# Packed attention with a top-1 mixture of experts: whole-row w1 loads, a new step order and a root on another engine in the first batch

## The chip, the cores and the metric

One core of a Trainium2 chip runs the kernel. The metric is device time in microseconds (us), from the first to the last instruction with what lies around them; the median of the runs counts.

## The reference

```python
def sm_attn(qq, kk, vv):                      # per batch and head
    s = scale * np.matmul(qq, kk.transpose(0, 1, 3, 2))
    s = s - np.max(s, axis=-1, keepdims=True)
    a = np.exp(s)
    a = a / (np.sum(a, axis=-1, keepdims=True) + 1e-09)
    return np.matmul(a, vv)
p_packed = sm_attn(p, k, v)                   # 32 packed rows
out = sm_attn(q, p_packed, p_packed)
# q, k, v: 8 batches x 8 heads x 576 x 64; p: 8 x 8 x 32 x 64
x = out as rows [4608, 512]
xn = x / (norm(x) + 1e-06);  en = emb / (norm(emb) + 1e-06)
logits = xn @ en.T / tau                      # 8 experts
expert = argmax(logits);  gate = softmax(logits)[expert]
out[row] = gate * (relu(x @ w1[expert]) @ w2[expert])
# w1: 8 x 512 x 1024, w2: 8 x 1024 x 512
```

## The kernel before

The kernel goes through eight batches of 576 rows. For each batch it computes the packed attention in two steps (att1: 32 packed rows per head against all keys, packed into the small matrices T, ppx and p1T; att2: the 576 queries against the 32 packed rows), and then one FFN with the one expert that `guess` finds for the whole batch. The expert's index is read into a register, and the loads of that expert's w1 (`load_w1`) and w2 (`load_w2`) are issued with it, by SyncE (SP) in batch 0 and by GpSimd (POOL) later on. Rows that chose another expert are counted (`gates_main`), and are computed again at the end only if there are any. Attention and FFN are folded together: since att2's result is a product of a softmax and packed rows, w1 is first multiplied with the packed rows (G, of heads in two groups of four), and the hidden layer is then a product of G with the softmax AT (`hidden`, items f0 to f7 for each half of the rows, first half hf=0). Matrices are kept in two parts, high and low (the low one is what rounding leaves), so that a product takes three passes at full speed; in batch 0's first half, `hidden` takes fp32 operands (g32, ats) directly.

The order of instructions on every engine is the order in which the program writes them (a manual schedule); generators are stepped by the FFN's loop. From batch 1 on, the FFN of batch b steps the attention of batch b+1 by a rule. In batch 0 a table of strings sets it: after item n of the FFN the letters of PLAN[n+1] are run, where q is a step of the start (`begin`), s a step of batch 0's own softmax, a a step of batch 1's attention, G a split of G into its parts on GpSimd, w a split of w2, r a step of batch 0's routing and g a step of its gates. `begin` loads the first batch, computes the guess early from a total, issues w1 and prefetches the following inputs on SP's queue. In it, the steps of batch 0's softmax follow two strings: ORDS, an order of steps (U unpack, B maximum, S shift, X exponential, T total, N normalise, R turn, H high half, L low half; 0 and 1 are the two halves of rows), and ENG, an engine for each of the steps S0, S1, N0, N1 and so on (v VectorE, p GpSimd).

Names and lines that matter below (numbers of the kernel before, and behind a stroke those of the changed one):

- L174/L175: inputs q, k, v on SP; L527/L530: the index into a register; L737/L743, L746: w1's DMAs; L745/L754: w2's DMAs.
- L815/L833: the products of w1 with the packed rows (`rows_w1`); L847/L852, L873: the items of `hidden`; L851, L852: their evacuation into hT by ScalarE and VectorE.
- L891/L920: the FFN's last product, 96 of it to the end of a batch, and L875/L904 its remainder of 64 rows.
- L410/L419 and L424/L433: turn and logits of the packed rows of batch 1, through T (L481/L484, VectorE); L514/L517: its guess on TensorE; L251/L260: scores; L780/L789: rows of w1 of the next batch.
- L554, L559, L565, L574 to L576, L580, L589, L599 (L557, L562, L568, L577 to L579, L583, L592, L602): the steps of att2's softmax on VectorE: unpack, maximum, shift, total, normalise, turn, low half. ScalarE takes the exponential (L568/L571) and the high half (L595).
- L651/L659: routing products, of the high and low halves with ppx; ScalarE (L667) and VectorE (L660) evacuate.
- L98 to L113: one Newton step of a reciprocal root, called `rsqrt`; L710, L711 (L718, L719) end it for the gates, L713 (L721) is the reciprocal that follows, on VectorE.

The guess of batch 1 (letter a) sets when GpSimd may issue its w1, and w2 follows three steps of att2 later:

```python
yield from guess(x, 2 if b > 1 else 0)
load_w1(x, x.e, queue=nc.gpsimd)
second = att2(x, keys_main(b + 1) if b else None, b == 0, b < 1)
if b:
    for _ in range(3):
        yield next(second)
    load_w2(x, x.e, nc.gpsimd)
yield from second
```

## Time and profile before

| | |
|---|---|
| median of 3 runs | 448.43 us (448.02 to 448.60) |
| profiled execution | 448.61 us |
| its span, first to last instruction | 447.0 us |
| mean clock granted to TensorE | 0.993 |
| busy: TensorE, VectorE, ScalarE, GpSimd | 431.6, 306.7, 203.3, 145.4 us |
| HBM read and written | 78.00 MB, 9.44 MB |

The span is that of one profiled execution, and all positions are microseconds from its first instruction. Busy time says how much an engine did; where the kernel can become shorter is told by the chain that ended last (which follows, from the last instruction backward, what released each step) and by the timelines of single engines, which give idle time and what ended it.

### The profile page before, as it was taken

Reading aid. Unit: us, or ns where it says so; the run is one execution under the profiler, and the core shown is the slowest. Engines: PE = TensorE matmul, PEld = TensorE weight load, DVE = VectorE, ACT = ScalarE, POOL = GpSimd, SP = SyncE. Lnnn points to the kernel's source line nnn. Section 1 sums busy time; section 2 is a strip of 40 time slices with the busy share of each in tenths; the row PEclk is TensorE's granted clock in tenths of the full one; section 3 lists DMA queues with packets and bytes.
Section 4 is the critical chain, followed back from the end, with each engine's and each line's share of the span. In section 5 each row is a group of like instructions: output and inputs, shape, how many; then the busy total and the mean of one; then the engine's idle time right before and its main releaser. Section 6 shows DMA issues by size and latency. Waiting matters only on the chain.

```text
span 447.0 us, 10448 instructions
## 1 busy us (share of the span) xinstructions
PE 431.6 (97%) x3762; PEld 340.7 (76%) x3763; DVE 306.7 (69%) x1020; ACT 203.3 (45%) x477; POOL 145.4 (33%) x184
## 2 busy tenths in 40 slices
PE   7789989999999999999999999999999999999994
PEld 5537768789687968879687887879787886879784
DVE  4478778569883799459894699658994598535400
ACT  2456723475137722476226742377234751466110
POOL 2446733153404422043503423044401534035000
PEclk9999999999999999999999999999999999999998
DMA  7999979856994379933996279934799306500011
GB/s 213 277 278 279 241 208 339 260 126 166 297 352 137 107 217 363 293 105 91 289 374 183 78 207 332 316 102 111 229 366 271 87 1 210 226 26 23 15 48 54
DMA packets 40843, 88.22 MB, mean 197 GB/s; under 512 B 10376, under 2 KB 19912, under 8 KB 40784
## 3 DMA queue, kind: packets, MB, share of 16 engines
q1 hardware_dynamic: 32496, 57.96, 45.4%
q0 software_dynamic: 8000, 29.43, 18.0%
q8 instruction: 32, 0.52, 0.5%
q14 instruction: 27, 0.22, 0.2%
q10 hardware_dynamic: 288, 0.08, 0.1%
HBM read 78.00 MB, written 9.44 MB: 196 GB/s over the span
## 4 chain that ended last, share of the span: by engine, by line
PE 90%; DMA 5%; SPq 1%; DVE 1%; ACT 1%; issue 0%; ACTq 0%
PE pf L891 41%; PE pf L847 23%; PE pf L875 7%; PE pt L651 7%; PE pt L251 4%; PE pt L780 3%; PE pt L381 3%; DMA nat<-in_q 2%; PE pt L361 2%; DMA w1t<-in_moe_w 2%; DMA nat<-in_v 2%; SPq L737 1%; PE pu L424 0%; ACT p L346 0%; PE pu L410 0%
## 5 line engine op out<-in xcount | busy, mean ns | idle before, releaser
L891 PE MATMUL pf<-w2s,hT 128*128 128x512 f32 (+1 forms) x792 | 190.0, 392 | 0.0
L891 PEld LDWEIGHTS pf<-w2s,hT 128*128 128x128 f32 x792 | 143.7, 190 | 38.1 <-issue 6.7
L756 POOL TENSOR_TENSOR w2s<-w2r,w2s 128x512 fp32r<-128x512 f32 x64 | 82.7, 1294 | 185.9 <-ACT w2s L755 185.3
L847 PE MATMUL pf<-AT,G 128*128 128x288 f32 x720 | 104.8, 299 | 0.0
L847 PEld LDWEIGHTS pf<-AT,G 128*128 128x128 f32 x720 | 97.6, 188 | 4.5 <-issue 2.8
L851 ACT ACTIVATE hT<-pf 128x224 fp32r<-128x224 f32 (+1 forms) x128 | 48.0, 388 | 46.0 <-PE pf L847 45.4
L852 DVE SCALAR_TENSOR_TENSOR hT<-pf,hT 128x224 fp32r<-128x224 f32 (+1 forms) x128 | 52.2, 411 | 15.2 <-ACT hT L851 14.8
L667 ACT ACTIVATE at<-pt 128x512 f32<-128x512 f32 (+1 forms) x40 | 23.9, 598 | 44.4 <-DVE lg L660 44.1
L755 ACT CAST w2s<-w2r 128x512 fp32r<-128x512 f32 x64 | 39.8, 624 | 1.2 <-issue 1.2
L1146 ACT ACTIVATE o<-pf,gate 128x512 f32<-128x512 f32 (+1 forms) x41 | 25.9, 635 | 30.1 <-PE pf L891 18.6
L651 PEld LDWEIGHTS pt<-ppx,AT 128*128 128x128 f32 (+1 forms) x240 | 33.0, 177 | 4.3 <-DVE p1T L375 0.4
L651 PE MATMUL pt<-ppx,AT 128*128 128x264 f32 (+1 forms) x240 | 35.5, 286 | 0.0
L660 DVE TENSOR_REDUCE lg<-pt 128x8 f32<-128x16 f32 (+1 forms) x40 | 6.8, 171 | 39.7 <-PE pt L651 39.7
L875 PE MATMUL pf<-w2r,h 128*64 128x256 f32 x256 | 33.9, 390 | 0.0
L281 DVE STREAM_TRANSPOSE kt<-nat 128x512 f32<-128x512 f32 x28 | 31.1, 1109 | 0.0
L794 DVE TENSOR_TENSOR G<-pt,G 128x512 fp32r<-128x512 f32 x28 | 18.8, 689 | 14.2 <-ACT G L793 14.2
L266 POOL TENSOR_TENSOR ppx<-pp,ppx 128x256 fp32r<-128x256 f32 x16 | 12.0, 773 | 40.5 <-ACT ppx L265 40.5
L568 ACT ACTIVATE st<-st 128x576 f32<-128x576 f32 (+1 forms) x17 | 11.2, 657 | 29.3 <-DVE st L565 28.6
L875 PEld LDWEIGHTS pf<-w2r,h 128*64 128x64 f32 x256 | 15.8, 136 | 9.9 <-issue 4.3
L745 POOL DMA_DIRECT2D w2r<-in_moe_w x28 | 19.8, 713 | 0.0
L595 ACT CAST AT<-at 128x576 fp32r<-128x576 f32 x16 | 10.7, 673 | 19.6 <-DVE at L589 19.6
L793 ACT CAST G<-pt 128x512 fp32r<-128x512 f32 x28 | 15.8, 588 | 7.1 <-DVE G L794 4.8
(172 smaller groups left out, 477.2 us busy)
## 6 DMA issues: line engine op xcount, KB each, us to landing
nat<-in_k SPq DMA_DIRECT2D x112, 140.0 KB, 3.3
nat<-in_q SPq DMA_DIRECT2D x112, 140.0 KB, 4.0
w1t<-in_moe_w POOLq DMA_DIRECT2D x14, 1024.0 KB, 7.3
w2r<-in_moe_w POOLq DMA_DIRECT2D x28, 512.0 KB, 10.6
out<-o SPq DMA_DIRECT2D x27, 256.0 KB, 2.8
nat<-in_v SPq DMA_DIRECT2D x32, 160.0 KB, 4.2
nat<-in_v SPq DMA_DIRECT2D x32, 128.0 KB, 4.1
w1t<-in_moe_w SPq DMA_DIRECT2D x8, 256.0 KB, 5.3
```

The costliest lines, as they stand in the source:

```text
L281: nc.vector.transpose(kt[:, :512].rearrange("p (c i a) -> p c a i", a=4, i=32), t[:, :16].rearrange("p (c a) d -> p c a d", a=4),)
L651: nc.tensor.matmul(pt[:r, 512 * g : 512 * g + XW], AT[:, a, g, c * P : c * P + r], x.ppx[:, m, g], start=(i == 0), stop=(i == 2),)
L667: nc.scalar.activation(scr[:r, :, : HB * D], ptv[:r, :, 0 : HB * D], AF.Square, accum_out=ss[:r, c : c + 1])
L745: queue.dma_start(t, w2e[:, 2 * i : 2 * i + 2, :])
L755: nc.scalar.copy(t[:, 0], raw)
L756: nc.gpsimd.tensor_tensor(out=t[:, 1], in0=raw, in1=t[:, 0].bitcast(F32), op=ALU.subtract)
L847: nc.tensor.matmul(pf[:, :HS], w, r, start=(n == 0), stop=(n == len(ops) - 1))
L851: nc.scalar.activation(hT[:, 0, f, cs], pf[:, :n], AF.Relu)
L852: nc.vector.scalar_tensor_tensor(out=hT[:, 1, f, cs], in0=pf[:, :n], scalar=0.0, in1=hT[:, 0, f, cs].bitcast(F32), op0=ALU.max, op1=ALU.su ...
L875: nc.tensor.matmul(pf[64 * hf : 64 * hf + 64, :256], h4[:, f], x.w2r[f // 2][:, f % 2, hf * 256 : hf * 256 + 256], start=(f == 0), stop=(f ...
L891: nc.tensor.matmul(pf[:, :w], hT[:, a, f, c * P : (c + 1) * P], x.w2s[f][:, m, at : at + w], start=(f == 0 and i == 0), stop=(f == NF - 1 ...
L1146: nc.scalar.activation(o[:, :w], pf[:, :w], AF.Copy, scale=x.gate[:, c : c + 1])
```

## The change

1. `load_w1` of batch 0 takes w1 as four DMAs of whole rows (128 x 1024, 512 KB each) instead of eight of half rows (256 KB each). One DMA of batch 1's keys (HELD) moves from ahead of the index load to behind w1's.
2. `rows_w1` goes by head group instead of by half of the columns. After group 0, four items of `hidden` (f0 to f3) are opened: their products with group 0 alone run first, in four banks of PSUM; then group 1 follows in a bank of another pool, and `hidden` adds the second products.
3. Batch 0's softmax: ORDS ends with H1 L1 H0 L0, and N1 moves from VectorE to GpSimd.
4. A new PLAN. Batch 0's row logits stand between L904's; T of batch 1 is copied ahead of its gates; more of L920 stands around the logits of batch 1 and ahead of its scores.
5. `att1` turns batch 1's second group one step later. `att2` of batch 1 runs its routing from inside (`early`), step by step in turn with the keys of batch 2, where before routing followed the keys.
6. `gates` takes an engine; for batch 0 its root (`rsqrt`, and the two operations behind it) goes to GpSimd.

```diff
+                if isinstance(b, int) and (b, n, e, h) == HELD:
+                    hold.append(move)
+                else:
+                    move()
...
+    HELD = (1, 1, 1, 1)
...
-    def att2(x, after=None, first=False, b1=False):
+    def att2(x, after=None, first=False, early=False):
...
+            if early:
+                steps = route(x)
+                yield next(steps)
+                low(1)
+                yield
+                yield from alternate(steps, after)
+                return
             yield
             low(1)
             yield from idle(2)
-
-        if b1:
-            yield from alternate(softmax(), after)
-        else:
-            yield from softmax()
             if after:
                 yield from after
...
-    def gates(x):
+    def gates(x, eng=nc.vector):
...
-        for n, _ in enumerate(rsqrt(ss, y, "g")):
+        for n, _ in enumerate(rsqrt(ss, y, "g", eng)):
             if n % 3 == 2:
                 yield
-        nc.vector.tensor_tensor(out=y, in0=y, in1=ss, op=ALU.mult)
-        nc.vector.tensor_scalar(out=y, in0=y, scalar1=1e-6, scalar2=None, op0=ALU.add)
+        eng.tensor_tensor(out=y, in0=y, in1=ss, op=ALU.mult)
+        eng.tensor_scalar(out=y, in0=y, scalar1=1e-6, scalar2=None, op0=ALU.add)
         yield
         nc.vector.reciprocal(y, y)
...
-        for hf in range(2):
-            for i in range(parts):
...
+        for i in range(NPR if whole else 2):
+            if whole:
+                queue.dma_start(w1t[:, i], w[:, i])
...
+        def rows_w1(g):
+            if g == 0:
+                for _ in range(2):
+                    x.g32.append(sb.tile([P, NG, 512], F32, name="g32", tag="w2s", bufs=NF))
+                pfs = [ps.tile([P, 512], F32, name="pf", tag="pf") for _ in range(2)]
+                order = [(fc, (2 * a, 2 * a + 1)) for a in range(2) for fc in range(2)]
+            else:
+                pt = pb.tile([P, 1024], F32, name="pt", tag="pb")
+                pfs = [pt[:, fc * 512 : fc * 512 + 512] for fc in range(2)]
+                order = [(fc, range(HB)) for fc in range(2)]
...
+        def first_half(f, g):
+            if g == 0:
+                opened[f] = ps.tile([P, 512], F32, name="pf", tag="pf")
+            nc.tensor.matmul(
+                opened[f][:, :HS], x.g32[f // 4][:, g, f % 4 * P : f % 4 * P + P],
+                x.ats[0][:, g], start=(g == 0), stop=(g == NG - 1),
+            )
...
-            for fc in range(2):
-                yield from rows_w1(fc)
+            yield from rows_w1(0)
+            for f in range(HB):
+                first_half(f, 0)
+            yield
+            yield from rows_w1(1)
...
-        second = att2(x, keys_main(b + 1) if b else None, b == 0, b < 1)
+        second = att2(x, keys_main(b + 1) if b else None, b == 0, b == 1)
...
-        if b:
+        if b > 1:
             yield from route(x)
...
-        load_w1(x, x.e, NPR)
+        load_w1(x, x.e, True)
+        hold.pop()()
...
-        yield from gates(x)
+        yield from gates(x, nc.vector if b else nc.gpsimd)
...
-    ORDS = "U0a B0a S0a X0a U0b B0b T0a S0b X0b T0b N0a N0b U1 R0a B1 S1 X1 R0b T1 N1 R1 H0 H1 L1 L0"
-    ENG = "pvpvppppvp"
+    ORDS = "U0a B0a S0a X0a U0b B0b T0a S0b X0b T0b N0a N0b U1 R0a B1 S1 X1 R0b T1 N1 R1 H1 L1 H0 L0"
+    ENG = "pvppppppvp"
...
-        "qssq", "sssssssssq", "ssqsssG", "ss", "", "ss", "sa", "asss", "a", "Gsq",
+        "qssq", "sssssssss", "sss", "ss", "sGs", "ss", "Gs", "ssa", "ssa", "qa",
...
```

Where instructions go is seen from each engine's own order. First TensorE at the start of batch 0's FFN (pf and pt are PSUM banks, at and g the fp32 softmax and G). Before:

```order
L815 MATMUL pf<-w1t,tw 32x512 x16
L847 MATMUL pf<-at,g_502 128x288 x8
L847 MATMUL pf<-at,g_530 128x288 x2
L424 MATMUL pu<-enT,T 64x8 x4
L847 MATMUL pf<-at,g_530 128x288 x6
L847 MATMUL pf<-AT,G 128x288 x12
```

And in the changed kernel:

```order
L833 MATMUL pf<-w1t,tw 32x512 x8
L852 MATMUL pf<-at,g_472 128x288 x4
L833 MATMUL pt<-w1t,tw 32x512 x8
L852 MATMUL pf<-at,g_472 128x288 x4
L852 MATMUL pf<-at,g_473 128x288 x8
L873 MATMUL pf<-AT,G 128x288 x12
```

Four products of the items, with group 0, now stand between the two halves of the w1 rows, and the logits (L424) have left this place.

Second, TensorE around the scores and the routing of batch 1, in the middle of the last product of batch 0's FFN. Before:

```order
L891 MATMUL pf<-w2s,hT 128x512 x6
L410 MATMUL pu<-ident,pp_966 128x128
L410 MATMUL pu<-ident,pp_968 128x128
L891 MATMUL pf<-w2s,hT 128x512 x3
L424 MATMUL pu<-enT,T 64x8 x4
L514 MATMUL pu<-m_1015,itau 1x8 x2
L251 MATMUL pt<-kt,T 32x288 x16
L891 MATMUL pf<-w2s,hT 128x512 x69
L651 MATMUL pt<-ppx,AT 128x264 x12
```

And in the changed kernel:

```order
L920 MATMUL pf<-w2s,hT 128x512 x6
L419 MATMUL pu<-ident,pp_961 128x128
L419 MATMUL pu<-ident,pp_963 128x128
L920 MATMUL pf<-w2s,hT 128x512 x6
L433 MATMUL pu<-enT,T 64x8 x4
L920 MATMUL pf<-w2s,hT 128x512 x3
L517 MATMUL pu<-m_1009,itau 1x8 x2
L260 MATMUL pt<-kt,T 32x288 x16
L920 MATMUL pf<-w2s,hT 128x512 x48
L659 MATMUL pt<-ppx,AT 128x264 x6
L920 MATMUL pf<-w2s,hT 128x512 x6
L659 MATMUL pt<-ppx,AT 128x264 x6
```

Six more products (12 and 3 instead of 9 in all ahead of the scores) stand around the logits L433, and the first routing product stands behind 48 of the last product instead of 69.

Third, GpSimd, from the last w1 DMA of batch 1 on. Before, where the root of batch 0's gates is on VectorE:

```order
L737 DMA w1t<-in_moe_w 128x4x512
L745 ISA
L745 DMA w2r<-in_moe_w 128x2x512
L745 ISA
L745 DMA w2r<-in_moe_w 128x2x512
L745 ISA
L745 DMA w2r<-in_moe_w 128x2x512
L745 ISA
L745 DMA w2r<-in_moe_w 128x2x512
L644 MEMSET lg 64x8
L645 MEMSET ss 64x1
```

And in the changed kernel, from the root's third operation of the last Newton step on (the two w1 DMAs and the two operations ahead of it are not shown):

```order
L112 TENSOR_SCALAR rq_t<-rq_t 128x5
L113 TENSOR_TENSOR gy<-rq_t,gy 128x5
L754 ISA
L754 DMA w2r<-in_moe_w 128x2x512
L754 ISA
L754 DMA w2r<-in_moe_w 128x2x512
L754 ISA
L754 DMA w2r<-in_moe_w 128x2x512
L754 ISA
L754 DMA w2r<-in_moe_w 128x2x512
L718 TENSOR_TENSOR gy<-gy,ss 128x5
L719 TENSOR_SCALAR gy<-gy 128x5
```

The root's last two operations (L718, L719) stand behind all DMA issues of batch 1's weights; nine operations of the root stand ahead of the index load.

Fourth, VectorE at the start of batch 1's softmax. Before:

```order
L554 STREAM_TRANSPOSE st<-pt 128x288 x2
L710 TENSOR_TENSOR gy<-gy,ss 128x5
L711 TENSOR_SCALAR gy<-gy 128x5
L559 TENSOR_REDUCE mx_1087<-st 128x18
L565 TENSOR_TENSOR st<-st,mx_1087 128x576
L554 STREAM_TRANSPOSE st<-pt 128x288 x2
L559 TENSOR_REDUCE mx_1094<-st 128x18
L713 RECIPROCAL gy<-gy 128x5
L714 TENSOR_TENSOR lg<-lg,gy 128x40
L574 TENSOR_REDUCE s_1099<-st 128x18
```

And in the changed kernel:

```order
L557 STREAM_TRANSPOSE st<-pt 128x288 x2
L562 TENSOR_REDUCE mx_1091<-st 128x18
L721 RECIPROCAL gy<-gy 128x5
L722 TENSOR_TENSOR lg<-lg,gy 128x40
L568 TENSOR_TENSOR st<-st,mx_1091 128x576
L557 STREAM_TRANSPOSE st<-pt 128x288 x2
L729 TENSOR_REDUCE gate<-lg 128x5
L730 TENSOR_SCALAR gate<-gate 128x5
L562 TENSOR_REDUCE mx_1114<-st 128x18
L732 RECIPROCAL gate<-gate 128x5
```

The reciprocal that takes the root's result (L713, now L721) came behind both maxima and now comes behind the first; shift and unpack of the second half stand behind it.

## Rows read from the trace of the kernel before

**Rows 1.** The page of the profile, its parts on the engines (busy time, share of the span, instructions) and the chain that ended last (shares of the span by engine):

```profile
PE 431.6 (97%) x3762; PEld 340.7 (76%) x3763; DVE 306.7 (69%) x1020; ACT 203.3 (45%) x477; POOL 145.4 (33%) x184
...
PE 90%; DMA 5%; SPq 1%; DVE 1%; ACT 1%; issue 0%; ACTq 0%
```

**Rows 2.** The chain that ended last, from 8 to 32 us: start in us, length in us, what ran (SPq is SyncE's queue):

```profile
9.22 8.44 DMA nat<-in_q
17.68 0.31 SPq L174
...
18.04 0.47 SPq L527
...
19.01 0.38 SPq L737
...
22.76 7.06 DMA w1t<-in_moe_w
```

**Rows 3.** The timeline of TensorE from 22 to 40 us: start, length (of all that are counted in xN), line, operation, shapes, and in brackets the idle time before it and what ended it:

```profile
23.29 1.06 PE L815 MATMUL pf<-w1t,tw 64*32 64x512 f32 x8
...
30.85 5.12 PE L847 MATMUL pf<-at,g 128*128 128x288 f32 x20
...
36.57 3.18 PE L847 MATMUL pf<-at,g 128*128 128x288 f32 x12 [0.27 <-ACT m L434]
```

**Rows 4.** The timeline of VectorE from 24 to 40 us, same columns:

```profile
26.85 0.44 DVE L589 STREAM_TRANSPOSE at<-st 128x288 f32<-128x288 f32 x1
...
30.90 0.76 DVE L580 TENSOR_TENSOR st<-st,s 128x576 f32<-128x576 f32 x1
```

**Rows 5.** The timeline of GpSimd from 8 to 40 us, same columns (the first two rows are the first and the last of 14 operations of the embeddings' root, one behind the other):

```profile
9.83 0.18 POOL L103 TENSOR_TENSOR rq_t<-rq_h,rq_i 8x1 f32<-8x1 f32 x1 [3.76 <-DVE rq_i L93]
...
13.32 0.20 POOL L139 TENSOR_SCALAR enrm<-enrm 8x1 f32<-8x1 f32 x1
...
25.23 0.67 POOL L580 TENSOR_TENSOR st<-st,s 128x288 f32<-128x288 f32 x1 [0.42 <-DVE s L576]
...
29.27 1.26 POOL L266 TENSOR_TENSOR G<-g,G 128x512 fp32r<-128x512 f32 x1
```

**Rows 6.** The timeline of TensorE from 57 to 66.5 us, same columns:

```profile
61.25 0.95 PE L891 MATMUL pf<-w2s,hT 128*128 128x512 f32 x3
63.29 0.41 PE L424 MATMUL pu<-enT,T 128*64 128x8 f32 x8 [1.10 <-DVE T L481]
63.98 0.24 PE L514 MATMUL pu<-m,itau 128*1 128x8 f32 x4 [0.28 <-DVE m L434]
...
65.28 1.84 PE L891 MATMUL pf<-w2s,hT 128*128 128x512 f32 x4
```

**Rows 7.** Windows of 1 us: busy time in all and of PE, PEld, DVE, ACT and POOL (instructions), the clock granted to TensorE (1.00 is 2.4 GHz), the DMA engines' share and GB/s:

```profile
65.00:66.00 1.00, 1.00 (x18) 0.63 (x3) 0.93 (x6) 0.00 (x0) 0.00 (x0) 0.79 0.73 200
66.00:67.00 1.00, 1.00 (x4) 0.74 (x3) 0.96 (x5) 0.00 (x0) 0.57 (x1) 0.50 0.01 4
...
68.00:69.00 1.00, 1.00 (x3) 0.78 (x3) 0.97 (x4) 0.68 (x1) 1.00 (x3) 0.50 0.77 143
69.00:70.00 1.00, 1.00 (x6) 0.78 (x5) 0.96 (x4) 0.00 (x0) 1.00 (x2) 1.00 1.03 418
```

**Rows 8.** The chain that ended last, over the whole span, its longer pieces: start, length, what ran:

```profile
65.35 17.79 PE pf L891 x69
83.14 1.48 PE pt L651 x12
...
90.48 2.99 PE pf L891 x12
...
116.47 16.24 PE pf L891 x69
```

**Rows 9.** The timeline of TensorE from 82 to 94 us, columns as in rows 3:

```profile
88.53 1.95 PE L780 MATMUL pt<-w1t,T 64*32 64x512 f32 x32 [0.33 <-ACT at L667]
```

**Rows 10.** The timeline of GpSimd from 60 to 75 us, columns as in rows 3:

```profile
66.43 1.58 POOL L737 DMA_DIRECT2D w1t<-in_moe_w  x2 [1.95 <-DVE gy L710]
68.00 2.83 POOL L745 DMA_DIRECT2D w2r<-in_moe_w  x4
70.88 0.10 POOL L644 MEMSET lg<- 64x8 f32 x1
```

**Rows 11.** The timeline of VectorE from 63 to 82 us, same columns:

```profile
64.76 0.14 DVE L521 CAST gi<-idx 1x1 f32<-1x1 uint32 x1
...
67.32 0.76 DVE L565 TENSOR_TENSOR st<-st,mx 128x576 f32<-128x576 f32 x1
...
69.54 0.18 DVE L713 RECIPROCAL gy<-gy 128x5 f32<-128x5 f32 x1
...
75.11 0.69 DVE L599 TENSOR_TENSOR AT<-at,AT 128x576 fp32r<-128x576 f32 x1
...
78.02 0.76 DVE L599 TENSOR_TENSOR AT<-at,AT 128x576 fp32r<-128x576 f32 x1 [0.74 <-ACT AT L595]
...
79.19 0.40 DVE L276 STREAM_TRANSPOSE kt<-nat 128x256 f32<-128x256 f32 x1
```

**Rows 12.** The view of the cores: span and mean clock granted to TensorE:

```profile
core 0: 447.0 us, clock 0.993
```

More of the change, by code (lines that the diff above doesn't have):

```diff
@@ L451, in pack @@
             turned = []
-            def turn(g):
+            for g in range(NG):
                 turned.append(pb.tile([P, 1024], F32, name="pt", tag="pb"))
                 p1_turn(x, g, turned[g], turned[g][:, 512:])
-            turn(0)
-            if tight:
-                turn(1)
-            yield from idle(gap)
-            if not tight:
-                turn(1)
+                if g == 0:
+                    yield
             for g in range(NG):
@@ L630, in softmax @@
             yield from idle(2)
-        if b1:
-            yield from alternate(softmax(), after)
-        else:
-            yield from softmax()
             if after:
                 yield from after
+        yield from softmax()
     def route(x):
@@ L806, in ffn @@
         h4 = sb.tile([P, NF, 64], F32, name="h4", tag="h4")
-        def rows_w1(fc):
-            fs = slice(fc * 512, fc * 512 + 512)
-            pfs = [ps.tile([P, 512], F32, name="pf", tag="pf") for _ in range(NG)]
-            for g in range(NG):
-                for c in range(HB):
-                    h = head(g, c)
+        def rows_w1(g):
[4 more added lines that the diff above has]
+                order = [(fc, (2 * a, 2 * a + 1)) for a in range(2) for fc in range(2)]
+            else:
+                pt = pb.tile([P, 1024], F32, name="pt", tag="pb")
+                pfs = [pt[:, fc * 512 : fc * 512 + 512] for fc in range(2)]
+                order = [(fc, range(HB)) for fc in range(2)]
+            for fc, hs in order:
+                for h in hs:
+                    c = head(g, h)
                     nc.tensor.matmul(
-                        pfs[g][32 * c : 32 * c + 32],
+                        pfs[fc][32 * c : 32 * c + 32],
                         half_rows(x.Tw, h)[:, g * P + 32 * c : g * P + 32 * c + 32],
-                        half_rows(x.w1t[:, 2 * g + h // 2], h)[:, fs],
+                        half_rows(x.w1t[:, 2 * g + h // 2], h)[:, fc * 512 : fc * 512 + 512],
                         start=True,
@@ L845, in hidden @@
                 ]
-            for n, (w, r) in enumerate(ops):
-                nc.tensor.matmul(pf[:, :HS], w, r, start=(n == 0), stop=(n == len(ops) - 1))
+                for n, (w, r) in enumerate(ops):
+                    nc.tensor.matmul(pf[:, :HS], w, r, start=(n == 0), stop=(n == len(ops) - 1))
             yield
@@ L863, in ffn @@
         if late:
-            for fc in range(2):
-                yield from rows_w1(fc)
+            yield from rows_w1(0)
+            for f in range(HB):
+                first_half(f, 0)
+            yield
+            yield from rows_w1(1)
         elif not hasattr(x, "w1g"):
```

36 lines of the change are left out of this document (16 added, 20 removed), and 3 rows, old and new, of the table PLAN.

## The prediction

> **What bounds the kernel now.** I read the page's shares first: TensorE is busy for 97% of the span and carries 90% of the chain that ended last [rows 1]. So what counts is time in which TensorE idles, or runs at the lower clock. The long pieces of that chain then show where: from batch 1 on, a batch repeats every 51.2 us with hardly a gap, and the change touches nothing there. What is left is batch 0 and the attention of batch 1 that runs beside its FFN, from 9 to 93.5 us.
>
> Three stretches have slack. First, the load: the chain goes from in_q's landing (9.22 + 8.44 = 17.66) over SP's index load to the w1 issues and ends with the landing of the last w1 piece at 22.76 + 7.06 = 29.82 [rows 2]; TensorE waits for w1 piece by piece until then, and the FFN's first item starts at 30.85 [rows 3]. Second, around 63 us: 1.10 us of idle before the row logits (for the T copy) and 0.28 us before the guess [rows 6]. Third, behind that idle time the granted clock stands at 0.50 from 66 to 69 us, the lower of the two levels (1.2 of 2.4 GHz) [rows 7]: the x69 stretch of the last product takes 17.79 us, where the same x69 in batch 1 takes 16.24 [rows 8]. That fall cost 1.55 us. All times below are on the clock of the profiled execution before (448.61 us with what lies around its 447.0 us span, 0.18 above the median of the runs), unless "after the early gain" is said.
>
> **The change, part by part.**
>
> *w1 as four whole-row DMAs, index load moved past one key DMA.* SP now reaches the w1 issue with the key DMA held back. Before, the index load began at 18.04 and the w1 issues came from 19.01 on, 8 of them until 22.76 [rows 2]. Four issues of the same kind, two of which together replace four of the old ones, are out by about 20. SP still has to wait for the DMA slot that in_q frees at 17.66, so the start comes earlier by at most the 19.01 - 18.25 = 0.75 us that the held DMA and its queue slot took. The bytes are the same 2 MB. I expect the last w1 at 28.3, some 1.5 us earlier: 0.75 from the start and as much from fewer, longer rows. The bounds: 29.8 (nothing gained) and 27.3.
>
> *By head group, with four items opened.* Products of group 0 need two of the four DMAs; then TensorE waits for the first half of the attention, that DVE turns at 26.85 + 0.44 = 27.29 [rows 4]. Four half items of 0.512 us (5.12 / 10; the trace shows two records to a product) [rows 3] run until 29.3, the eight products of group 1 (1.06 for four, and denser behind each other) until 31.1, and the other four halves until 33.1. Then the second half's attention (R1) is due. Its N1 moves from DVE, 0.76 us, to GpSimd, where 288 columns take 0.67, so two of them 1.35, behind the split of G at 1.26 (which comes at about 30.0) [rows 4, 5]: R1 ends at 33.4, and with the evacuation f4 can start at 33.85. Eight products of 0.512 end at 38.0. Before, the sixteen ended at 36.57 + 3.18 - a rest = 39.4 [rows 3], of which 0.41 was the logits of batch 0, that now stand later; there they cover a stall of 0.27. So the early part gains 39.4 - 38.0 - 0.41 + 0.27 = **1.3 us**. Bounds: 0.5, if w1 lands no earlier than before (group 1 then ends at 31.9), and 2.2, if GpSimd's N1 comes before the split.
>
> *The row logits of batch 1.* The T copy comes ahead of the gates' root on DVE and six more products stand in the idle time (15 instead of 9 of the 96 before the key scores). I get the end of the scores at 64.95 instead of 65.28, with 6 products of 16.24 / 69 = 0.235 us [rows 8] more done: 0.33 + 1.41 = 1.74 us gained. The clock then has no idle time to fall after, 1.55 us; and the 0.33 us that TensorE waited for an evacuation ahead of the weight rows at 88.53 [rows 9] is covered by products that now lie between the routing steps. Together 3.6 us, if nothing else moves.
>
> *The gates' root on GpSimd.* This is the part that decides. On GpSimd nine of the root's operations come first, then the index, two w1 DMAs, four more root operations, four w2 DMAs, and only then the last two, for which DVE's reciprocal waits. The index is ready at 64.76 + 0.14 on DVE [rows 11]; GpSimd's first w1 issue followed at 66.43, two took 1.58 and the four of w2 2.83 [rows 10]. Its next instruction, a memset, begins at 70.88, right at the end of the fourth (68.00 + 2.83): so GpSimd works through the issues one after the other and nothing passes them. In the new order the index is as early as before within 0.15 us, so the first issue begins at 66.3 and ends the second at 67.9. Four root operations at 0.27 each (14 of them took from 9.83 to 13.52 [rows 5]) make 69.0, the four issues 71.8, the last two operations 72.4.
>
> On DVE the reciprocal stands behind the first three operations of the softmax of batch 1, at 66.6, so DVE stands idle for about 5.8 us. Behind it are the shift, the second half's turn and maximum, that had been done ahead of it before (67.32 to 69.54 = 2.2 us), and then the chain that took from 69.54 to the end of the first low half at 75.11 + 0.69 = 75.80 (6.26 us), and to 78.02 + 0.76 = 78.78 for the second [rows 11]. 72.4 + 2.2 + 6.3 = 80.9 for the first low half. TensorE has 48 products after the scores: 64.95 + 48 x 0.235 = 76.25. Then comes the first routing product, which needs that low half. **TensorE waits 4.7 us**, until 81.0. Nothing else is in its queue that could run.
>
> After such a wait I expect what the rows of before show after 1.10 + 0.28 us of idle time: the clock at the lower level for some 3 us, 1.55 us lost [rows 6, 7]. I take 1.7; bounds 0 (it doesn't fall) and 2.6 (longer at the lower level, since what follows, 6-product groups between routing steps, is less dense than the x69).
>
> What is left from there: 33 products (7.8), 30 records of routing at 1.48 / 12 = 0.123 (3.7), the weight rows at 1.9 [rows 8, 9]: 13.35. The end of batch 0's part is 81.0 + 13.35 + 1.7 = 96.1 instead of 90.48 + 2.99 = 93.47: **2.6 us lost**. From there the kernel goes as before.
>
> *Edits that I cost at nothing:* the T of the first attention steps and the turn of batch 1 one step later, since the next of TensorE's products are in its queue beside them; and the keys of batch 2, spread between routing steps instead of standing ahead of them: DVE turned them from 79.19 on [rows 11], while the scores of batch 2 come only after the last product at 93.47; they now come some 5 to 10 us later, still ahead of that. If that cover were gone, TensorE would wait for them once, up to 1 us.
>
> **Sum:** -1.3 + 2.6 = +1.3 us, from the profile's 448.61 to 449.9, and from the median of 448.43 to **449.7 us**.
>
> **Rivals.**
>
> A. *The DMA issues don't hold GpSimd up.* If GpSimd is through six issues at little cost, the root's end comes 66.3 + 4 x 0.27 + 0.5 = 67.9, DVE waits 1.3 us, the first low half is there at 67.9 + 8.5 = 76.4, and TensorE runs through: it gains the 1.3 + 1.74 + 1.55 + 0.33 = 4.9, which makes 443.5. The point from which this decides: the root's end before 67.8 costs nothing; each microsecond later is one lost; with the clock's fall the change breaks even where it comes at 71.0. The rows speak against it: 0.7 to 0.8 us per issue and the memset only behind the last [rows 10]. The Trainium skill, "DMA: Bandwidth & Descriptors", section "Anatomy of one DMA — SWDGE (gpsimd) path", would have it this way: dispatch of some 50 ns, and descriptor generation "small, variable"; by it, an estimate, six issues take well under 1 us and the sum would be about 443.5 as well. The trace does not agree, with 2.83 us for four. Chance 0.11.
>
> B. *TensorE waits, but the clock does not fall,* or only for the few tenths in which little runs. The price of 1.7 is gone: 448.0, no change that can be told. For it: the granted clock is 0.993 over the whole span [rows 12], so the many other waits of TensorE did not make it fall. Against it: [rows 6, 7] fell after a shorter one. Also in this case lies a mean of A and the forecast, by 1 us less waiting on DVE since part of the shift's chain can overlap with ScalarE. Chance 0.27, a third of it under 447.5.
>
> C. *Slower still:* the early part gains nothing, because the held key DMA and w1's long rows share the DMA engines until 29.8, or because TensorE's short wait for R0 (26.6 to 27.3) makes the clock fall too, on a stretch that is on the chain. 449.7 + 1.3 to 449.7 + 2.1: 451.0 to 451.8. Chance 0.14.
>
> D. *The change doesn't do what it says:* w1 comes earlier but its use is set by R0 and R1 on DVE and GpSimd, so that early w1 buys less than I wrote, 0.5 instead of 1.3: 450.5. It counts with the forecast.
>
> **How the numbers follow.** The forecast has 0.48 (D within it), A 0.11, B 0.27, C 0.14. What a measurement of this kernel can tell from no change is 0.2%, 0.9 us: faster is under 447.5, slower over 449.3. Faster: A and a third of B, 0.20. Same: the rest of B and 0.10 of the forecast (where the fall costs 1.2 or less), 0.28. Slower: 0.38 + 0.14 = 0.52. The range takes in B down to 446.8 and C up to 451.8 and leaves out A and some of B. The likeliest case's own range is 449.0 to 450.8.
>
> **What would show it.** In the changed kernel: last w1 by 28.5 and four half items before 29.5; f4's start bound by DVE's evacuation of R1; no idle time before L433 of batch 1; a gap of 5 us and more on DVE ended by GpSimd before L721; on GpSimd L719 behind four L754 issues; a gap of 4 to 5 us on TensorE before the first L659 of batch 1, and 0.50 in the clock's rows behind it. If the gap on DVE is under 2 us, the forecast is wrong, and the step that failed is the issues' cost on GpSimd; if it is there and TensorE's gap is not, I have the place of the low half's need wrong.

## The result, and the profile after

The changed kernel takes 450.98 us (median of 7 runs, 449.62 to 451.85), the kernel before 448.04 us beside it (445.08 to 448.60). The ratio is 1.0076, 95% interval 1.0052 to 1.0099: slower by 2.3 to 4.4 us. The forecast was 449.7, range 446.8 to 451.8.

The profiled execution is the shortest of the seven (449.62 us, span 447.9). A second one, taken later, has a span of 448.8. The last product's long stretch in batch 1, which began at 116.47 before [rows 8], begins 1.9 us later in the one and 2.5 us later in the other. (The spans are only 0.9 and 1.8 us longer than the 447.0 before, in part because the profiled execution before has one later batch of 51.65 us, where its other batches take 51.2 to 51.3.) The chain that ended last, the first and the second execution of the changed kernel:

```profile
118.36 16.22 PE pf L920 x69
```

```profile
118.98 16.22 PE pf L920 x69
```

GpSimd's timeline of the changed kernel, from w1's issues on, answers to [rows 10]:

```profile
65.44 1.61 POOL L746 DMA_DIRECT2D w1t<-in_moe_w  x2 [1.20 <-issue]
...
67.95 0.20 POOL L113 TENSOR_TENSOR gy<-rq_t,gy 128x5 f32<-128x5 f32 x1
68.53 2.93 POOL L754 DMA_DIRECT2D w2r<-in_moe_w  x4 [0.38 <-issue]
71.48 0.21 POOL L718 TENSOR_TENSOR gy<-gy,ss 128x5 f32<-128x5 f32 x1
71.78 0.23 POOL L719 TENSOR_SCALAR gy<-gy 128x5 f32<-128x5 f32 x1
```

Two w1 issues take 1.61 us, four w2 issues 2.93 (1.58 and 2.83 before), and the root's last two operations begin right where the fourth issue ends. L719 ends at 72.01.

VectorE's timeline answers to [rows 11]:

```profile
72.04 0.19 DVE L721 RECIPROCAL gy<-gy 128x5 f32<-128x5 f32 x1 [5.96 <-POOL gy L719]
...
79.79 0.69 DVE L602 TENSOR_TENSOR AT<-at,AT 128x576 fp32r<-128x576 f32 x1
...
82.70 0.76 DVE L602 TENSOR_TENSOR AT<-at,AT 128x576 fp32r<-128x576 f32 x1 [0.74 <-ACT AT L598]
```

From 66.08 on it waits for L719, 5.96 us. The low halves (L602) then end at 80.48 and 83.46; before they ended at 75.80 and 78.78.

TensorE's timeline answers to [rows 6]:

```profile
61.75 0.41 PE L433 MATMUL pu<-enT,T 128*64 128x8 f32 x8
...
64.28 11.42 PE L920 MATMUL pf<-w2s,hT 128*128 128x512 f32 x48
79.48 0.51 PE L659 MATMUL pt<-ppx,AT 128*128 128x264 f32 x2 [3.78 <-ACT AT L598]
80.54 1.25 PE L659 MATMUL pt<-ppx,AT 128*128 128x264 f32 x4 [0.54 <-DVE AT L602]
81.58 2.45 PE L920 MATMUL pf<-w2s,hT 128*128 128x512 f32 x6
...
86.03 1.56 PE L920 MATMUL pf<-w2s,hT 128*128 128x512 f32 x6
...
92.24 3.06 PE L920 MATMUL pf<-w2s,hT 128*128 128x512 f32 x12
95.13 0.95 PE L873 MATMUL pf<-AT,G 128*128 128x288 f32 x6
```

The 1.10 and 0.28 us of idle time around the row logits (L433) are gone, as is the 0.33 of [rows 9]. In their place TensorE waits 3.78 us for the first routing product, whose last step ahead of it is ScalarE's high half, and 0.54 us more for VectorE's low half. The six products at 81.58 take 2.45 us, those at 86.03 only 1.56. Why, the windows of 1 us show (columns as in [rows 7]; the clock is the third number from the right):

```profile
80.00:81.00 1.00, 0.46 (x2) 0.47 (x3) 1.00 (x2) 0.00 (x0) 0.00 (x0) 0.56 0.00 0
81.00:82.00 1.00, 1.00 (x5) 0.92 (x5) 0.92 (x2) 0.01 (x1) 0.00 (x0) 0.50 0.00 0
...
83.00:84.00 1.00, 1.00 (x6) 0.82 (x5) 0.97 (x4) 0.62 (x2) 0.00 (x0) 0.73 0.00 0
84.00:85.00 1.00, 1.00 (x9) 0.96 (x8) 0.20 (x3) 0.32 (x2) 0.00 (x0) 1.00 0.57 131
```

The clock falls to 0.50 behind the wait, as it fell before behind the shorter one.

The start of batch 0's FFN on TensorE answers to [rows 3]:

```profile
22.12 3.09 PE L833 MATMUL pf<-w1t,tw 64*32 64x512 f32 x16 [0.27 <-DMA w1t<-in_moe_w]
25.93 2.18 PE L852 MATMUL pf<-at,g 128*128 128x288 f32 x8 [0.72 <-ACT g L843]
...
31.04 6.66 PE L852 MATMUL pf<-at,g 128*128 128x288 f32 x24 [0.68 <-ACT g L843]
...
45.49 0.71 PE L370 MATMUL pt<-ident,p 128*128 128x128 f32 x5
...
50.22 1.71 PE L659 MATMUL pt<-ppx,AT 128*128 128x264 f32 x12 [1.06 <-DVE p1T L384]
```

The first turn of batch 1 stands at 45.49 instead of 47.71, 2.2 us earlier. Then a wait that before did not have: 1.06 us for VectorE's copy of p1T. The first routing product of batch 0, at 51.27 before, starts at 50.22, in the second execution at 50.71. VectorE's timeline ahead of this copy (L384):

```profile
48.35 1.15 DVE L290 STREAM_TRANSPOSE kt<-nat 128x512 f32<-128x512 f32 x1
...
49.81 0.46 DVE L384 COPY p1T<-pt 64x128 f32<-64x128 f32 x2
```

### The profile page after: what moved, and what is told of

Read it like the earlier page. It is cut to its first block, busy times and chain, and to the rows that moved or that the text cites. A ratio compares the mean times of both kernels' runs of the same rounds, so it can differ in the third digit from the quotient of the medians.

```text
span 447.9 us, 10440 instructions
## 1 busy us (share of the span) xinstructions
PE 430.7 (96%) x3762; PEld 340.9 (76%) x3763; DVE 304.9 (68%) x1007; ACT 203.3 (45%) x477; POOL 149.2 (33%) x200
## 4 chain that ended last, share of the span: by engine, by line
PE 89%; DVE 3%; DMA 3%; issue 1%; POOL 1%; ACT 1%; SPq 0%; POOLq 0%; ACTq 0%
PE pf L920 38%; PE pf L873 21%; PE pt L659 7%; PE pf L904 7%; PE pt L260 3%; PE pt L789 3%; PE pt L390 3%; PE pf L852 2%; PE pt L370 2%; DMA pn<-in_p 1%; DMA w1t<-in_moe_w 1%; PE pt L238 1%; DMA nat<-in_v 1%; PE pf L833 1%; PE pt L833 1%
## 5 line engine op out<-in xcount | busy, mean ns | idle before, releaser
L920 PE MATMUL pf<-w2s,hT 128*128 128x512 f32 (+1 forms) x792 | 189.9, 391 | 0.0
L920 PEld LDWEIGHTS pf<-w2s,hT 128*128 128x128 f32 x792 | 143.0, 189 | 37.5 <-issue 6.7
L659 PE MATMUL pt<-ppx,AT 128*128 128x264 f32 (+1 forms) x240 | 36.6, 289 | 5.4 <-ACT AT L598 3.8
L659 PEld LDWEIGHTS pt<-ppx,AT 128*128 128x128 f32 (+1 forms) x240 | 33.6, 180 | 10.6 <-ACT AT L598 4.2
L904 PE MATMUL pf<-w2r,h 128*64 128x256 f32 x256 | 34.1, 390 | 0.0
L904 PEld LDWEIGHTS pf<-w2r,h 128*64 128x64 f32 x256 | 15.8, 136 | 9.7 <-issue 4.3
```

What stands on the lines that cost most here:

```text
L659: nc.tensor.matmul(pt[:r, 512 * g : 512 * g + XW], AT[:, a, g, c * P : c * P + r], x.ppx[:, m, g], start=(i == 0), stop=(i == 2),)
L904: nc.tensor.matmul(pf[64 * hf : 64 * hf + 64, :256], h4[:, f], x.w2r[f // 2][:, f % 2, hf * 256 : hf * 256 + 256], start=(f == 0), stop=(f ...
L920: nc.tensor.matmul(pf[:, :w], hT[:, a, f, c * P : (c + 1) * P], x.w2s[f][:, m, at : at + w], start=(f == 0 and i == 0), stop=(f == NF - 1 ...
```

## The experiments

Each run was timed in five rounds beside the kernel before. Theory Q, which they test: VectorE stands behind a root that GpSimd ends only after six DMA issues, the low half comes late, and TensorE waits. Rival O: the loss lies in the new order of TensorE's steps and in the early part.

| run | median us | ratio to before, 95% interval |
|---|---|---|
| root_on_vector | 444.32 | 0.9924 (0.9894 to 0.9953) |
| root_ahead_of_issues | 444.64 | 0.9918 (0.9891 to 0.9945) |
| w2_issues_behind_root | 446.69 | 0.9966 (0.9945 to 0.9987) |
| reciprocal_behind_low_half | 444.61 | 0.9921 (0.9894 to 0.9948) |
| changed_again | 450.95 | 1.0073 (1.0048 to 1.0098) |
| early_part_alone | 446.81 | 0.9969 (0.9946 to 0.9992) |
| late_part_alone | 446.63 | 0.9971 (0.9946 to 0.9996) |
| root_on_vector_turn_as_before | 444.43 | 0.9915 (0.9885 to 0.9945) |
| before_with_root_on_gpsimd | 452.19 | 1.0093 (1.0057 to 1.0130) |
| logits_and_turn_as_before | 444.40 | 0.9922 (0.9893 to 0.9951) |
| n1_on_vector_too | 444.82 | 0.9940 (0.9917 to 0.9964) |
| wait_filled_with_products | 449.93 | 1.0054 (1.0033 to 1.0075) |

**The engine: the root back on VectorE** (root_on_vector)

```diff
-        yield from gates(x, nc.vector if b else nc.gpsimd)
+        yield from gates(x, nc.vector)
```

> The changed kernel with the gates' root of batch 0 on VectorE again, all else as changed. Theory Q (VectorE stands behind a root that GpSimd ends only after six DMA issues, and TensorE then waits for the low half): the gap of 5.96 us on VectorE and the 4.3 us on TensorE at 76 to 80.5 are gone, the fall of the clock behind them (1.5 us) too; 5.8 us under the changed kernel, about 445.2 us, faster than before by 2.5 to 3. Rival O (the loss lies in the new order of routing and in the early part): 450 us or more. Rival C (the clock falls anyway): about 446.7.

Measured: 444.32. VectorE's timeline of this run:

```profile
66.09 0.17 DVE L719 TENSOR_SCALAR gy<-gy 128x5 f32<-128x5 f32 x1
...
66.83 0.18 DVE L721 RECIPROCAL gy<-gy 128x5 f32<-128x5 f32 x1
...
74.58 0.70 DVE L602 TENSOR_TENSOR AT<-at,AT 128x576 fp32r<-128x576 f32 x1
```

The root ends at 66.26 on VectorE with no wait, the low half at 75.28, and TensorE goes from the 48 products into routing without a gap:

```profile
76.11 0.89 PE L659 MATMUL pt<-ppx,AT 128*128 128x264 f32 x6
```

The clock does not fall there. Rival O is out: everything else of the change is in this kernel, which is 3.4 us faster than before by its ratio.

**The queue, not the engine** (root_ahead_of_issues): the last Newton step and the two operations behind it are stepped ahead of the index load.

```diff
-        "", "aa", "g", "ag", "gaaa", "gaa", "ga", "ga", "ag", "ag",
+        "", "aa", "g", "ag", "gggaaa", "aa", "a", "ga", "ag", "ag",
```

> The root stays on GpSimd, but its last Newton step and the two operations behind it are issued ahead of the index load, so that all six DMA issues come behind it and about 1.6 us later. Theory Q: the root ends near 66 us instead of 72.0, VectorE's gap is under 0.5 us, TensorE runs through: about 445.2 us. If GpSimd as the engine is at fault (slow small operations), not the queue: no better than 449. Rival O: 450 or more.

Measured: 444.64, the same as on VectorE. GpSimd in this run:

```profile
66.86 0.23 POOL L719 TENSOR_SCALAR gy<-gy 128x5 f32<-128x5 f32 x1
...
68.42 1.62 POOL L746 DMA_DIRECT2D w1t<-in_moe_w  x2 [1.03 <-issue]
```

It ends the root at 67.09 us, and its six issues then begin at 68.42 instead of 65.44 (1.3 of these 3.0 us come from the early part of this execution). Nobody waits for them: TensorE's timeline lists no idle time from 52 to 100 us. So the slower small operations (0.20 to 0.24 us here) cost nothing: it was their place behind the issues.

**Which issues** (w2_issues_behind_root): w2's four issues come three steps later.

```diff
-            for _ in range(3):
+            for _ in range(6 if b == 1 else 3):
                 yield next(second)
             load_w2(x, x.e, nc.gpsimd)
```

> As changed, but the four w2 issues of batch 1 come three steps later, behind the root's last two operations; w1's two issues stay ahead of the last Newton step. Theory Q: the root ends at 72.0 - 2.9 - 0.4 = 68.7 us, VectorE waits 2.7 us instead of 5.96 and TensorE about 1.0 instead of 4.3: 446 to 448 us, the upper end if the clock still falls behind the shorter wait. If the issues cost GpSimd little and the index is what is late: no change, 450 to 451.

Measured: 446.69, in the stated interval. VectorE, and then TensorE, in this run:

```profile
70.03 0.19 DVE L721 RECIPROCAL gy<-gy 128x5 f32<-128x5 f32 x1 [2.73 <-POOL gy L719]
...
77.79 0.70 DVE L602 TENSOR_TENSOR AT<-at,AT 128x576 fp32r<-128x576 f32 x1
```

```profile
77.49 0.51 PE L659 MATMUL pt<-ppx,AT 128*128 128x264 f32 x2 [0.56 <-ACT AT L598]
78.54 0.76 PE L659 MATMUL pt<-ppx,AT 128*128 128x264 f32 x4 [0.54 <-DVE AT L602]
```

VectorE's wait is 3.23 us shorter than in the changed kernel (2.73 against 5.96), TensorE's 3.22 us shorter (0.56 + 0.54 against 3.78 + 0.54). One to one: from the root's end on there is no slack. Behind 1.10 us of waiting the clock stayed at 1.00 in every window from 78 to 82 us.

**Who stands behind the wait** (reciprocal_behind_low_half): GpSimd's order as changed, VectorE's part of the gates written behind the first low half.

```diff
-        "", "aa", "g", "ag", "gaaa", "gaa", "ga", "ga", "ag", "ag",
-        "a", "a", "a", "a", "a", "a", "a", "a", "", "",
+        "", "aa", "g", "ag", "gaaa", "gaa", "ga", "aaa", "aaa", "aaa",
+        "aggg", "a", "", "", "", "", "", "", "", "",
```

> GpSimd's order is as in the changed kernel, root behind the issues and ending at 72.0 us; only VectorE's part of the gates (the reciprocal that waits for it and what follows) is written behind the first low half of batch 1's softmax. Theory Q: nothing waits for the late root, low half at 75 us, TensorE runs through: about 445.2 us. If the lateness of the gates themselves costs (ScalarE's stores wait for them and hold PSUM banks): 448 or more.

Measured: 444.61. VectorE in this run:

```profile
73.44 0.69 DVE L602 TENSOR_TENSOR AT<-at,AT 128x576 fp32r<-128x576 f32 x1
...
74.71 0.18 DVE L721 RECIPROCAL gy<-gy 128x5 f32<-128x5 f32 x1
```

The root is as late as ever (L719 ends at 72.73), and costs nothing, since the reciprocal stands where it has already come. The gates themselves are not urgent; what waited was the softmax queued behind them.

**A second execution of the changed kernel** (changed_again)

> The changed kernel once more, for a second profiled execution beside fresh runs. Theory Q: VectorE's gap of 5.9 to 6.0 us and TensorE's two waits of 4.3 us in all are there again; the clock stands at 0.50 for 3.4 us behind them. The median was 450.98 and the profiled execution 449.62 with a clock of 0.993, others 0.989 and 0.991: where this execution is longer, a second stretch at 0.50 of 3.4 us will be found, near 17 us or directly behind the first. About 450.5.

Measured: 450.95. TensorE waits 3.78 and 0.54 us again, and the clock is at 0.50 from 80.94 to 84.35 us in place of 80.13 to 83.54. The second fall that I looked for is not in this trace either. It is in those of root_ahead_of_issues, w2_issues_behind_root and before_with_root_on_gpsimd, at 17.3 us for 3.4 us. What it costs the changed kernel is left open. The first two of these three have the changed early part, and they begin batch 0's first routing product at 51.50 and 51.46 us, the five other executions with that part at 50.22 to 51.10. The third has the early part of before, and begins it at 51.28, as before.

**The early part alone** (early_part_alone): the changed kernel with `att1`, `att2`, `gates` and the call of `route` as before, and PLAN's tail from the 23rd string on as before, except for the two letters q of the later row logits.

```diff
-        "aawa", "awa", "aq", "", "q", "arwrw", "", "ara", "arraar", "ararrrw",
-        "", "aa", "g", "ag", "gaaa", "gaa", "ga", "ga", "ag", "ag",
+        "aawa", "awa", "qg", "", "q", "arwrw", "", "ara", "arraar", "ararrrgw",
+        "", "gaa", "agaaaag", "", "ragraaararga", "a", "gar", "gr", "", "rggr",
...
```

> The changed kernel with only its early part kept (w1 as whole rows, held key DMA, rows of w1 by head group, opened items, ORDS, ENG, the row logits of batch 0 later), the steps from batch 1's turn on as before, root on VectorE. The traces show the changed kernel 2.2 us ahead of before at the first turn of batch 1 (45.49 against 47.71) and 1.05 us ahead at the first routing product, after a new wait of 1.05 us for VectorE's copy of p1T. With the turn as before that wait should be gone: 448.3 - 1.9 = 446.4. If the prediction's size of the early part (1.3) is right: 447.0. Idle time and fall of the clock at 63 to 69 us stay as before.

Measured: 446.81, between the two numbers; the interval (0.4 to 2.4 us faster) holds both. Which of items 1, 2 and 3 of the change makes this gain, no run takes apart. The wait and the fall of the middle are there as before; TensorE in this run, where the row before showed 1.10:

```profile
62.51 0.41 PE L433 MATMUL pu<-enT,T 128*64 128x8 f32 x8 [1.12 <-DVE T L490]
```

The wait for p1T is gone, but 0.28 us for ScalarE's exponential and 0.59 us for GpSimd's ppx came in its place, ahead of the same routing product.

**The late part alone** (late_part_alone): the kernel before with the changed `att1`, `att2`, call of `route` and tail of PLAN, and the root on VectorE.

```diff
-        "awa", "g", "", "", "arwrw", "", "ara", "arraar", "ararrrgw", "",
-        "gaa", "agaaaag", "", "ragraaararga", "a", "gar", "gr", "", "rggr", "r",
+        "awa", "aq", "", "q", "arwrw", "", "ara", "arraar", "ararrrw", "",
+        "aa", "g", "ag", "gaaa", "gaa", "ga", "ga", "ag", "ag", "a",
...
```

> The kernel before with only the late part of the change: turn of batch 1 one step later, row logits of batch 1 among more products, routing of batch 1 beside the keys of batch 2, root on VectorE. The prediction's terms for it, 1.74 + 1.55 + 0.33 = 3.6 us, less up to 1.05 for the wait for p1T that the later turn makes: 448.3 - 2.6 to 3.6 = 444.7 to 445.7. Rival: routing in six groups among the products costs TensorE waits of its own and eats half: 446.5.

Measured: 446.63, above the interval that I gave by 0.9 us and near the rival's number. The trace has what was named: no idle time from 54 to 96 us, no fall, a wait of 1.22 us for p1T, and the x69 of batch 1 at 114.44, 2.0 us earlier than before. I had 2.6 to 3.6. Routing among the products brought no wait of its own in the trace, so the rival's reason is not borne out; the wait for p1T took 1.22 instead of 1.05 us, and the 1.74 us of the row logits was too much, as is shown below.

**The turn and the logits** (root_on_vector_turn_as_before, then logits_and_turn_as_before): on top of the root on VectorE, first `att1` as before, then batch 0's row logits and their split back among the items.

```diff
-            for g in range(NG):
-                turned.append(pb.tile([P, 1024], F32, name="pt", tag="pb"))
-                p1_turn(x, g, turned[g], turned[g][:, 512:])
-                if g == 0:
-                    yield
+            turn(0)
+            if tight:
+                turn(1)
...
-        "aawa", "awa", "aq", "", "q", "arwrw", "", "ara", "arraar", "ararrrw",
+        "aawa", "awa", "q", "", "q", "arwrw", "", "ara", "arraar", "ararrrw",
```

> The changed kernel with the root on VectorE and the turn of batch 1's second group where it was before, so that VectorE copies p1T ahead of the second key transpose and TensorE need not wait 1.05 us at 50 us. If that wait is on the chain: 444.3 - 0.8 to 1.05 = 443.3 to 443.5 (0.27 of it may come back as a wait for ScalarE's exponential ahead of the turn). If the wait is absorbed later: 444.3.

Measured: 444.43 against 444.32. TensorE in this run:

```profile
47.09 0.77 PE L370 MATMUL pt<-ident,p 128*128 128x128 f32 x5 [0.28 <-ACT p L355]
...
50.87 1.61 PE L665 MATMUL pt<-ppx,AT 128*128 128x264 f32 x11 [0.59 <-POOL ppx L275]
```

The 1.05 us are gone, 0.28 and 0.59 came instead: a gain of 0.2 us that the runs can't tell. The second of these two runs moves the letters q to where the logits stand among the items again:

```diff
-        "sq", "", "", "a", "awGG", "aa", "a", "w", "aw", "a",
-        "aawa", "awa", "q", "", "q", "arwrw", "", "ara", "arraar", "ararrrw",
+        "sq", "", "", "a", "awGG", "aa", "aq", "w", "aw", "a",
+        "qaawa", "awa", "", "", "", "arwrw", "", "ara", "arraar", "ararrrw",
```

> The changed kernel with the root on VectorE, the turn of batch 1 as before, and batch 0's row logits back among the items of the hidden layer (with the split of their result as early as before). In the run without the last of these TensorE waited 0.28 us for the exponential and 0.59 for GpSimd's ppx at 50.8 us in place of 1.05 for p1T. If ppx was late because of the logits, the 0.59 is gone: 0.5 to 0.6 under that run, about 443.8. If the 0.28 and something else keep it: no difference that can be told, 444.4.

Measured: 444.40. The 0.59 are gone, so ppx was late because of the logits; but there is 0.27 at 42.85, for the logits' own evacuation (the wait of [rows 3]), beside 0.27 for the exponential. The x69 of batch 1 begins at 112.49, against 112.74 with the root on VectorE alone. So the moves of logits and turn trade waits of 0.3 to 1.05 us for one another.

**N1** (n1_on_vector_too)

```diff
-    ENG = "pvppppppvp"
+    ENG = "pvpvppppvp"
```

> As the run beside it (root on VectorE, turn and logits as before), with N1 on VectorE again as well, 0.76 us there instead of 1.16 on GpSimd. The prediction held that R1 behind GpSimd's N1 sets the start of item f4; the traces show TensorE without idle time from 31.7 us to 46 us, so I now expect nothing: within 0.3 us of the run beside it. If the prediction's step is right: 0.4 us less.

Measured: 444.82 against 444.40 beside it, intervals that overlap: nothing, as expected. N1's engine is hidden.

**The root on GpSimd in the old order** (before_with_root_on_gpsimd): the kernel before with item 6 of the change alone.

```diff
-        yield from gates(x)
+        yield from gates(x, nc.vector if b else nc.gpsimd)
```

> The kernel before with only the gates' root of batch 0 on GpSimd. There too the root's last operations stand behind all six issues and end near 72.5 us, and VectorE's reciprocal waits for them, some 4 us. But TensorE has 69 products in its queue behind the scores instead of 48: it needs the low half at 83 us, and VectorE has it 6.3 us after the root, at 78.8. Theory Q (it is the place, not the engine): no wait on TensorE, and the T copy comes some 0.7 us earlier since VectorE has fewer small operations ahead of it: 447.3, or 445.8 if the clock then does not fall. Rival (the root on GpSimd costs 4 to 6 us wherever it stands): 450 or more.

Measured: 452.19, slower by 0.6 to 1.3%. My expectation failed. VectorE in this run, and TensorE:

```profile
72.95 0.19 DVE L713 RECIPROCAL gy<-gy 128x5 f32<-128x5 f32 x1 [4.71 <-POOL gy L711]
...
78.53 0.69 DVE L599 TENSOR_TENSOR AT<-at,AT 128x576 fp32r<-128x576 f32 x1
...
81.44 0.76 DVE L599 TENSOR_TENSOR AT<-at,AT 128x576 fp32r<-128x576 f32 x1 [0.74 <-ACT AT L595]
...
82.61 0.40 DVE L276 STREAM_TRANSPOSE kt<-nat 128x256 f32<-128x256 f32 x1
...
85.72 0.21 DVE L660 TENSOR_REDUCE lg<-pt 128x8 f32<-128x16 f32 x2
```

```profile
64.11 16.31 PE L891 MATMUL pf<-w2s,hT 128*128 128x512 f32 x69
...
81.72 0.86 PE L891 MATMUL pf<-w2s,hT 128*128 128x512 f32 x3
86.69 1.69 PE L651 MATMUL pt<-ppx,AT 128*128 128x264 f32 x6 [4.11 <-ACT at L667]
```

VectorE waits 4.71 us, as I had it, and the low half is there at 79.2 us, ahead of the routing product at 80.26, as I had it too. But TensorE waits 4.11 us ahead of the third group of routing products (86.69), which has no free bank: the evacuation of the first on VectorE (L660, 85.72; ScalarE's L667 begins right behind it, at 85.95) stands behind twelve key transposes (82.61 to 85.72), and those stand behind the late softmax. In this wait the clock falls to 0.50, at 85.5 us, and stays there until 92.4, twice as long as in the changed kernel. I had looked only at the first thing behind the wait. In the changed kernel routing and keys alternate, and this place is safe; the first routing product isn't.

**The clock** (wait_filled_with_products): 15 products that nothing reads run while TensorE waits.

```diff
+                    if late and (c, f) == (2, 4):
+                        busy = ps.tile([P, 512], F32, name="busy", tag="pf")
+                        for _ in range(15):
+                            nc.tensor.matmul(
+                                busy, hT[:, 0, 0, :P], x.w2s[0][:, 0], start=True, stop=True
+                            )
```

> The changed kernel with 15 more products of the last layer's kind (0.235 us each, 3.5 us, into a bank that nothing reads) on TensorE between the 48 products and the first routing product, in the 3.8 us in which it waits for the low half. VectorE and GpSimd run as in the changed kernel, so the low half comes no earlier. If the fall of the clock to 0.50 behind the wait comes from the idle time and costs what the rows say (six products 2.25 instead of 1.40 us, three 3.4 us long windows at half speed in all once): no fall near 81 us, 1.5 us less than the changed kernel, 449.4. Rival B' (the clock falls there for another reason, or the fall is hidden behind VectorE's low half): the same as the changed kernel, 450.9.

Measured: 449.93, ratio 1.0054 against 1.0073 of the changed kernel, so 0.8 to 1.0 us less, between the two numbers. The two intervals overlap; but the six runs (449.45 to 450.17) lie below all twelve of changed_again (450.28 to 452.64), and their mean granted clock is 0.994 to 0.999 against 0.986 to 0.993. TensorE in this run, and a window behind the wait:

```profile
76.59 3.76 PE L930 MATMUL busy<-w2s,hT 128*128 128x512 f32 x15
80.35 0.51 PE L659 MATMUL pt<-ppx,AT 128*128 128x264 f32 x2
81.40 0.76 PE L659 MATMUL pt<-ppx,AT 128*128 128x264 f32 x4 [0.54 <-DVE AT L602]
82.00 1.57 PE L920 MATMUL pf<-w2s,hT 128*128 128x512 f32 x6
...
85.24 1.01 PE L659 MATMUL pt<-ppx,AT 128*128 128x264 f32 x6 [0.24 <-ACT at L675]
...
95.19 0.95 PE L873 MATMUL pf<-AT,G 128*128 128x288 f32 x6
```

```profile
82.00:83.00 1.00, 1.00 (x7) 0.82 (x6) 0.79 (x2) 0.14 (x1) 0.00 (x0) 1.00 0.00 0
```

TensorE has no gap but the 0.54 and the 0.24, and the clock stays at 1.00; the six products at 82.00 take 1.57 us instead of 2.45. From the second L659 row to batch 1's first item it is 95.19 - 81.40 = 13.79 us, in the changed kernel 95.13 - 80.54 = 14.59. The fall is caused by the idle time, and it costs 0.8 us, not the 1.5 that I had written: at full clock TensorE comes so early to the third group that it waits 0.24 us for ScalarE, so a part of the fall was hidden. Most of the loss is the wait itself.

## Why the prediction was right, and where it was off

**The step that decided** was right in its mechanism, and each of its parts came out within 1 us. Forecast (less the 1.3 us of the early part where it is a position) and measured: four issues hold GpSimd, 2.83 and 2.93 us; root's end 72.4 - 1.3 = 71.1 and 72.0; VectorE's gap 5.8 and 5.96; TensorE's wait 4.7 and 4.32; end of batch 0's part 96.1 - 1.3 = 94.8 and 95.30. Three experiments each take away one link (engine, order of GpSimd, order of VectorE), and all three come out at 444.3 to 444.6; a fourth shortens the wait, and TensorE's wait shrinks with VectorE's, microsecond for microsecond.

**Rival A** (issues that cost GpSimd little) had the price of a change without the wait about 1 us too low: 443.5, where the runs without the wait show 444.3 to 444.6. And the issues do hold GpSimd, 0.7 to 0.8 us each [rows 10], and L718 started where the last one ended. The Trainium skill, "DMA: Bandwidth & Descriptors", section "Anatomy of one DMA — SWDGE (gpsimd) path", lists a dispatch of some 50 ns. For the engine that issues, this case's trace does not agree (1.61 us for two issues, 2.93 for four). **Rival B** was wrong in that the clock does fall; but the fall costs 0.8 to 1.0 instead of my 1.7, so about half of what this rival struck out was indeed not there. **Rival C's** amount (451.0 to 451.8) is what the median of 450.98 comes nearest to, just outside the likeliest case's own range of 449.0 to 450.8. Its reasons were not the ones: the clock was at 1.00 from 22 to 31 us, and TensorE waited for w1 only ahead of its first rows (0.27 us; those at 28.04 began without a wait). But that the early part gains next to nothing is near to what follows.

**The terms that were mis-sized.** The early part: 1.3 us forecast, 1.05 and 0.56 measured at the first routing product in the two executions. These two are the earliest of all: five more traces (root_on_vector, root_ahead_of_issues, w2_issues_behind_root, reciprocal_behind_low_half, wait_filled_with_products) are of kernels that do the same up to there, and they begin this product at 50.79 to 51.50. Over the seven it is from 1.05 us ahead of before to 0.23 us behind, 0.35 ahead in the median. At the first turn they are 0.95 to 2.2 us ahead, 1.5 in the median, about as forecast. What was gained there is lost to 1.04 to 1.08 us of waiting at a step that I had costed at nothing, "the turn of batch 1 one step later": VectorE's copy of p1T came to stand behind a second key transpose (two operations of 1.15 and 0.26 us), and holds the bank that routing needs. The sentence named TensorE's next products as the cover and not what stands ahead of the copy on VectorE. The step that I had used for N1 (R1 bounds f4) was wrong as well: R1 is turned by 32.23 us, and TensorE is busy without a gap from 31.04 to 45 us. It waits earlier: for VectorE's R0 in five of the seven traces (0.21 to 1.76 us), as I had it, but also for ScalarE's evacuation of G (0.68 to 0.71 us ahead of the second halves in all seven), that I hadn't named.

From the first routing product to the end of batch 0's part, 51.27 to 93.47, the forecast had 2.6 us more; the two executions show 2.9 and 3.0 more (45.08 and 45.23 against 42.20 us). With the early part that makes 1.8 and 2.5 at the end of batch 0's part, where the forecast had 1.3. The medians say 2.9 (2.3 to 4.4). With the 0.35 us of the early part that the seven traces show in the median, in place of 1.05 and 0.56, the sum is 2.5 to 2.7, inside that interval. So the forecast came out too low chiefly by the early part.

That the middle came out so close (2.6 and 2.9) is in part luck, since three sizes in it were off. First, the row logits: TensorE had 1.10 + 0.28 = 1.38 us of idle time there to fill [rows 6], so 1.74 could not be gained. From the first routing product to the products behind the scores it takes 14.06 us (50.22 to 64.28) with six more products than in the 14.01 before (51.27 to 65.28), a gain of 1.36. Second, the fall: 1.7 forecast, 0.8 to 1.0 measured. Third, a loss that the sum did not have: from 64.28 to batch 1's first item at 95.13 the changed kernel takes 30.85 us, root_on_vector 24.66 (64.85 to 89.51). Of these 6.2 us the waits that the timeline lists are 4.32 and the fall is 0.8; the other 1.1 us are not taken apart. The forecast's 4.7 + 1.7 = 6.4 for both was near their sum.

## What to carry to other kernels

When work moves to another engine, write down that engine's queue ahead of the result and the waiting engine's queue behind it, to the second and third item: here six DMA issues stood ahead, a softmax behind, and in the old order key transposes and then evacuations behind that. A result that nobody needs soon costs nothing if its consumer is written late, and everything if its consumer is written early on an in-order engine. Of two remedies, moving the work back and moving the consumer, both gave the whole loss back, 6.3 to 6.6 us.

## What the runs showed of the hardware

- Behind 4.3 us of idle time on TensorE the granted clock fell to 0.50 for 3.4 us (80.13 to 83.54); behind 1.4 us in before it did the same [rows 6, 7], behind 1.10 us in w2_issues_behind_root it did not, and in the wait of 4.11 us in before_with_root_on_gpsimd it fell for 6.8 us (85.5 to 92.4). Fifteen products that nothing reads in place of the idle time prevented the fall.
- The fall took 0.9 us from six products (2.45 against 1.57) and more from the products around them, but cost the kernel only 0.8 to 1.0 in all: without it TensorE waited 0.24 us for ScalarE.
- Each DMA issue of w1 or w2 held GpSimd for 0.7 to 0.8 us (1.61 us for two, 2.93 for four), and the next operation in its order began only behind them.
- A small operation of 128 x 5 takes 0.20 to 0.24 us on GpSimd, at about 0.28 us from one to the next, against mostly 0.12 to 0.17 on VectorE. The kernel's time was the same with the root on either engine (444.32 and 444.64 us).
